# Weight conversion from 64-bit to 32-bit words: the stored width of ScalarE's part, and the engine that clamps

## The chip, the cores and the metric

One core of a Trainium2 chip runs the kernel. The metric is device microseconds of one execution. The core's engines run side by side and meet at semaphores: TensorE (matmuls and transposes, called PE in the rows, PEld for its weight loads), VectorE (DVE), ScalarE (ACT), GpSimd (POOL) and SyncE (SP), whose queue issues most of the DMAs. Each engine works its own queue in order.

## The reference

Windowed attention, then two gated expert layers one behind the other, on 2304 tokens of width 512.

```python
def attention(q, k, v):            # 4 batches, 8 heads, 576 positions, 64 wide
    scores = q @ k.T / 8           # only 0 <= row - column < 64 is kept
    return softmax(scores) @ v     # then heads side by side: x is 2304 x 512

def moe(x, w_gate, w_val, w_out):  # 512 -> 1536 -> 512
    g = x @ w_gate
    return (g * sigmoid(g) * (x @ w_val)) @ w_out

def moe2(x, w_gate, w_val, w_out):
    return (sigmoid(x @ w_gate) * (x @ w_val)) @ w_out
```

All inputs are 64-bit floats where the host hands them over as such: the weights reach the kernel as pairs of 32-bit words (`wide`), and the kernel makes 32-bit floats of them itself.

## The kernel before

The tokens are cut into five tiles of 512, 384, 512, 512 and 384 (BLOCKS, in blocks of 128). For each layer, tile and chunk `fc` of 128 of the 1536 hidden columns there are three steps, counted by `g`: the gate product (L429, 12 matmuls into bank g), the value product (L429, 12 matmuls into bank v) and the out product of the chunk before (L441, 12 matmuls). All products are made with operands split in a higher and a lower part (three terms each). Between them ScalarE makes the gate (L696, Silu or Sigmoid), VectorE multiplies (L705), ScalarE rounds the higher part of h (L707) and VectorE subtracts to get the lower one (L621), without which the out product can't go on.

What else has to be done is hung on steps in three lists, `before`, `during` and `after` a step's product: the attention of the next tile's blocks (transposes, scores, masks L263, exponentials L279, normalisation L292 to L294, and the copies kt L217, early_q L211, x L328 and L331), and the weights' conversion. The kernel's own order within these lists is the order in which each engine gets its instructions. The start, before the first product, follows a list written by hand (START), in which `ca` is round_a, `cb` is round_b, `ch` and `cl` are the split of a weight; six conversions are done in it (`ca0` to `ca5`).

There are 72 conversions of 128 x 512 weights, 36 per layer. The first layer's are due while the first token tile is multiplied, one per step; the second layer's are spread over the third and fourth tiles. One conversion goes so. SP loads 512 KB of raw words (L359). ScalarE, in round_a, scales the lower words and stores them as 16-bit integers in the first of the four 16-bit parts of a pair (L377), and stores the absolute upper word in t (L380). VectorE, in round_b, one step later, makes the second 16-bit part from sign and a constant (L388), clamps t (L389), shifts it (L390) and adds the lower word (L391). Then SP may load the next raw tile into that buffer (there are four), out weights and the second layer's go to DRAM for later tiles, and split_hi (L411, ScalarE) and split_lo (L415, VectorE) make the two parts used by the products.

Of the kernel before, what the change touches and what calls it, by code (L numbers as in the profile page):

```python
# [8 lines left out]
FP32 = mybir.dt.float32  # L9
FP32R = mybir.dt.float32r  # L10
INT32 = mybir.dt.int32
UINT32 = mybir.dt.uint32
UINT16 = mybir.dt.uint16
ACTF = mybir.ActivationFunctionType
ALU = mybir.AluOpType
# [4 lines left out]
F64_LEAST = 2.0 ** -15  # L20
F64_MOST = 122816.0
# [18 lines left out]
def attention_moe_moe(  # L40
# [20 lines left out]
    nc = tc.nc  # L61
# [7 lines left out]
    scale = 1.0 / float(D) ** 0.5  # L69
# [269 lines left out]
    raws = {}  # L339
# [22 lines left out]
    def words_of(r):  # L362
        w = r.rearrange("p (f two) -> p f two", two=2)
        half = r.bitcast(UINT16).rearrange("p (f four) -> p f four", four=4)
        return w[:, :, 0], w[:, :, 1], half[:, :, 0], half[:, :, 1], half[:, :, 3]

# [3 lines left out]
    def round_a(key):  # L372
        t = t_p.tile([128, 512], INT32, tag="t", name="t")
        mids[key] = t
        if wide:
            lower, upper, first, _, _ = words_of(raws[key])
            nc.scalar.activation(  # L377
                out=first, in_=lower.bitcast(UINT32), func=ACTF.Copy, scale=2.0 ** -29
            )
            nc.scalar.activation(out=t.bitcast(FP32), in_=upper.bitcast(FP32), func=ACTF.Abs)  # L380

    def round_b(key, keep):
        r = raws.pop(key)
        t = mids[key]
        tf = t.bitcast(FP32)
        if wide:
            lower, _, _, second, fourth = words_of(r)
            nc.vector.tensor_scalar(second, fourth, 0x8000, 0x4000, ALU.bitwise_and, ALU.bitwise_or)  # L388
            nc.vector.tensor_scalar(tf, tf, F64_LEAST, F64_MOST, ALU.max, ALU.min)  # L389
            nc.vector.tensor_scalar(t, t, 3, None, ALU.logical_shift_left)  # L390
            nc.vector.tensor_tensor(out=t, in0=t, in1=lower, op=ALU.add)  # L391
        else:
            nc.vector.tensor_copy(tf, r)
        mids[key] = tf
        if keep:
            d = dram.tile([128, 512], FP32, name=f"k{key[0]}{key[1]}{key[2]}")
            nc.sync.dma_start(out=d, in_=tf)
            kept[key] = d
# [117 lines left out]
    for b in range(B):  # L516
# [4 lines left out]
        first = {1: 12, 2: 24, 3: 46}[b]  # L521
# [29 lines left out]
    def conv_b(j):  # L551
        round_b(convs[j][1], convs[j][1][1] == "o")
        raw_ahead(j + 1 + 4)

    for j, (s, key) in enumerate(convs[SPLIT_EARLY:], SPLIT_EARLY):
        at(during, s + 1, round_a, key)
        at(during, s + 2, round_b, key, key[0] == 1 or key[1] == "o")
        at(during, s + 2, raw_ahead, j + 1 + 4)
        if key[0] == 0:
            plan_split(s + 2, key)  # L560
# [32 lines left out]
    for t in range(NTL, 2 * NTL):  # L593
        for fc in range(FC):
            n, key = SPT * t + 3 * fc + 5, (1, "o", fc)
# [29 lines left out]
    with tc.manual_schedule():  # L625
# [4 lines left out]
        t = ps_m.tile([128, 512], FP32, tag="a3", name="warm")  # L630
# [8 lines left out]
        for step in LOADS.split():  # L639
# [31 lines left out]
            "lo": lambda i: x_lo(i, x_of(0), i * 128),  # L671
            "wm": lambda k: warm(k),
            "ca": lambda j: round_a(convs[j][1]),
            "cb": lambda j: conv_b(j),
            "ch": lambda j: split_hi(convs[j][1]),
# [9 lines left out]
        for T in range(2 * NTL):  # L685
            m = T // NTL
            t = ORDER2[T - NTL] if m else T
            n = TILES[t][1]
            for fc in range(FC):
# [7 lines left out]
                    out=s, in_=gps[:, 0:n], func=(ACTF.Silu, ACTF.Sigmoid)[m]  # L697
# [54 lines left out]
```

## Time and profile before

| | |
|---|---|
| Median of three runs | 1010.43 us (1010.13 to 1010.93) |
| Profiled execution, its own time | 1010.98 us |
| Its span, first to last instruction | 1009.2 us |
| TensorE busy | 984.6 us (98%) |
| VectorE busy | 516.4 us (51%) |
| ScalarE busy | 496.7 us (49%) |
| GpSimd busy | 4.1 us, 20 instructions |

Busy times are sums over one profiled execution. TensorE's matmuls are pipelined and their ends are modelled, so its busy share says when it had work, not how well it ran. Times in a time line are microseconds from the first instruction of the span.

### The profile page before, as it was taken

Reading aid. Unit: us, or ns where it says so; the run is one execution under the profiler, and the core shown is the slowest. Engines: PE = TensorE matmul, PEld = TensorE weight load, DVE = VectorE, ACT = ScalarE, POOL = GpSimd, SP = SyncE. Lnnn points to the kernel's source line nnn. Section 1 sums busy time; section 2 is a strip of 40 time slices with the busy share of each in tenths; the row PEclk is TensorE's granted clock in tenths of the full one; section 3 lists DMA queues with packets and bytes.
Section 4 is the critical chain, followed back from the end, with each engine's and each line's share of the span. In section 5 each row is a group of like instructions: output and inputs, shape, how many; then the busy total and the mean of one; then the engine's idle time right before and its main releaser. Section 6 shows DMA issues by size and latency. Waiting matters only on the chain.

```text
span 1009.2 us, 14684 instructions
## 1 busy us (share of the span) xinstructions
PE 984.6 (98%) x5621; PEld 847.7 (84%) x5621; DVE 516.4 (51%) x1181; ACT 496.7 (49%) x981; POOL 4.1 (0%) x20
## 2 busy tenths in 40 slices
PE   8899998999999999999999999999999999999998
PEld 6677777999878788888999888899988888888997
DVE  6899994554576777767555323223322222223322
ACT  6899994655676668657444322222222222222222
POOL 1000000000000000000000000000000000000000
PEclk7799999999999999999999999999999999999999
DMA  9647798773176666573644400020020002000100
GB/s 225 187 152 214 205 234 205 196 151 108 55 223 204 203 201 223 172 233 106 210 146 146 167 1 1 1 84 1 1 73 1 1 1 73 0 1 1 42 1 32
DMA packets 164982, 113.03 MB, mean 112 GB/s; under 512 B 102704, under 2 KB 139568, under 8 KB 164912
## 3 DMA queue, kind: packets, MB, share of 16 engines
q1 hardware_dynamic: 161264, 111.18, 38.1%
q10 hardware_dynamic: 3648, 0.92, 0.4%
q8 instruction: 44, 0.72, 0.3%
q14 instruction: 26, 0.21, 0.1%
HBM read 90.05 MB, written 27.53 MB: 117 GB/s over the span
## 4 chain that ended last, share of the span: by engine, by line
PE 80%; DVE 7%; ACT 7%; issue 3%; SPq 2%; DMA 1%; DVEq 0%; ACTq 0%
PE a L441 26%; PE g L429 26%; PE v L429 24%; ACT raw L377 2%; SPq L118 2%; ACT z L279 1%; DVE raw L388 1%; PE att L244 1%; PE att L318 1%; DVE t L390 1%; PE att L302 1%; DMA ks<-in_k_dram 1%; ACT L279 1%; DVE t L389 1%; DVE s L705 1%
## 5 line engine op out<-in xcount | busy, mean ns | idle before, releaser
L429 PE MATMUL g<-x,wg 128*128 128x512 f32 (+1 forms) x1440 | 319.5, 370 | 0.7 <-ACT x L328 0.7
L429 PE MATMUL v<-x,wv 128*128 128x512 f32 (+1 forms) x1440 | 317.6, 369 | 0.0
L429 PEld LDWEIGHTS g<-x,wg 128*128 128x128 f32 x1440 | 264.6, 189 | 38.0 <-ACT x L328 0.9
L429 PEld LDWEIGHTS v<-x,wv 128*128 128x128 f32 x1440 | 261.2, 188 | 33.0
L705 DVE TENSOR_TENSOR s<-s,v 128x512 f32<-128x512 f32 (+1 forms) x120 | 75.9, 632 | 314.7 <-PE v L429 303.6
L696 ACT ACTIVATE s<-g 128x512 f32<-128x512 f32 (+1 forms) x120 | 66.7, 556 | 304.1 <-PE g L429 303.6
L441 PE MATMUL a<-h,wo 128*128 128x512 f32 (+1 forms) x720 | 164.8, 377 | 6.3 <-DVE h L621 6.3
L441 PE MATMUL a<-wo,h 128*128 128x512 f32 x648 | 157.4, 390 | 0.0
L707 ACT ACTIVATE h<-s 128x512 fp32r<-128x512 f32 (+1 forms) x120 | 70.6, 588 | 169.4 <-DVE s L705 169.3
L441 PEld LDWEIGHTS a<-h,wo 128*128 128x128 f32 x720 | 131.2, 190 | 26.5 <-DVE h L621 7.6
L441 PEld LDWEIGHTS a<-wo,h 128*128 128x128 f32 x648 | 121.3, 188 | 24.2
L377 ACT ACTIVATE raw<-raw 128x512 uint16<-128x512 uint32 x72 | 98.0, 1361 | 0.0
L621 DVE TENSOR_TENSOR h<-s,h 128x512 fp32r<-128x512 f32 (+1 forms) x120 | 76.2, 635 | 3.2
L388 DVE TENSOR_SCALAR raw<-raw 128x512 uint16<-128x512 uint16 x72 | 53.9, 748 | 17.4 <-ACT raw L377 17.3
L279 ACT ACTIVATE z<-z,nm 128x128 f32<-128x128 f32 x144 | 55.8, 390 | 2.8 <-DVE nm L263 2.7
L101 DVE TENSOR_TENSOR x<-rx,x 128x512 fp32r<-128x512 f32 (+1 forms) x20 | 12.8, 639 | 84.3 <-ACT x L100 84.3
L391 DVE CUSTOM_DVE_ANT_0 t<-raw,t 128x1024 uint16<-128x1024 uint16 x72 | 49.9, 693 | 2.5
L380 ACT ACTIVATE t<-raw 128x512 f32<-128x512 f32 x72 | 51.1, 710 | 0.0
L415 DVE TENSOR_TENSOR wo<-stay,wo 128x512 fp32r<-128x512 f32 x60 | 41.1, 685 | 0.0
L411 ACT ACTIVATE wo<-stay 128x512 fp32r<-128x512 f32 x60 | 37.4, 623 | 0.0
L415 DVE TENSOR_TENSOR wo<-tw,wo 128x512 fp32r<-128x512 f32 x48 | 32.9, 686 | 5.7 <-ACT wo L411 5.7
L389 DVE TENSOR_SCALAR t<-t 128x512 f32<-128x512 f32 x72 | 33.3, 462 | 0.0
(84 smaller groups left out, 569.4 us busy)
## 6 DMA issues: line engine op xcount, KB each, us to landing
raw<-in_moe_w_gate_dram SPq DMA_DIRECT2D x24, 512.0 KB, 4.2
raw<-in_moe_w_val_dram SPq DMA_DIRECT2D x24, 512.0 KB, 4.3
raw<-in_moe_w_out_dram SPq DMA_DIRECT2D x24, 512.0 KB, 3.7
tw<-k0o SPq DMA_DIRECT2D x48, 256.0 KB, 4.2
v<-in_v_dram SPq DMA_DIRECT2D x29, 256.0 KB, 4.6
out_dram<-o SPq DMA_DIRECT2D x18, 256.0 KB, 2.3
k<-ks SPq DMA_DIRECT2D x10, 384.0 KB, 5.4
k0o<-t SPq DMA_DIRECT2D x12, 256.0 KB, 2.3
```

The costliest lines, as they stand in the source:

```text
L279: nc.scalar.activation(out=z[:, hp, :], in_=z[:, hp, :], func=ACTF.Exp, scale=-1.0, bias=nm[:, hp:hp + 1], accum_out=su[:, hp:hp + 1],)
L377: nc.scalar.activation(out=first, in_=lower.bitcast(UINT32), func=ACTF.Copy, scale=2.0 ** -29)
L380: nc.scalar.activation(out=t.bitcast(FP32), in_=upper.bitcast(FP32), func=ACTF.Abs)
L388: nc.vector.tensor_scalar(second, fourth, 0x8000, 0x4000, ALU.bitwise_and, ALU.bitwise_or)
L391: nc.vector.tensor_tensor(out=t, in0=t, in1=lower, op=ALU.add)
L415: nc.vector.tensor_tensor(out=w[:, 1], in0=mids.pop(key), in1=w[:, 0].bitcast(FP32), op=ALU.subtract)
L429: nc.tensor.matmul(out=ps[:, 0:n], lhsT=w[:, a, c, :], rhs=xt[:, b, c, 0:n], start=(j == 0), stop=(j == len(mm) - 1),)
L441: nc.tensor.matmul(out=acc[e][:, 0:n] if m == 0 else acc[e], lhsT=w[:, a, cols] if m == 0 else h[:, a, cols], rhs=h[:, b, 0:n] if m == 0 e ...
L621: nc.vector.tensor_tensor(out=h[:, 1, 0:n], in0=s, in1=h[:, 0, 0:n].bitcast(FP32), op=ALU.subtract)
L696: nc.scalar.activation(out=s, in_=gps[:, 0:n], func=(ACTF.Silu, ACTF.Sigmoid)[m])
L705: nc.vector.tensor_tensor(out=s, in0=s, in1=vps[:, 0:n], op=ALU.mult)
L707: nc.scalar.activation(out=h[:, 0, 0:n], in_=s, func=ACTF.Copy)
```

## The change

The lower words, scaled, are stored by ScalarE over the whole 32-bit lower word, as integers of 32 bits, instead of in its lower 16 bits. The clamp of the magnitudes is taken out of VectorE's part and done by GpSimd, right behind the absolute value, with the same two bounds. VectorE's remaining three instructions stay as they were.

```diff
     def words_of(r):
         w = r.rearrange("p (f two) -> p f two", two=2)
         half = r.bitcast(UINT16).rearrange("p (f four) -> p f four", four=4)
-        return w[:, :, 0], w[:, :, 1], half[:, :, 0], half[:, :, 1], half[:, :, 3]
+        return w[:, :, 0], w[:, :, 1], half[:, :, 1], half[:, :, 3]
...
         if wide:
-            lower, upper, first, _, _ = words_of(raws[key])
+            lower, upper, _, _ = words_of(raws[key])
             nc.scalar.activation(
-                out=first, in_=lower.bitcast(UINT32), func=ACTF.Copy, scale=2.0 ** -29
+                out=lower, in_=lower.bitcast(UINT32), func=ACTF.Copy, scale=2.0 ** -29
             )
-            nc.scalar.activation(out=t.bitcast(FP32), in_=upper.bitcast(FP32), func=ACTF.Abs)
+            tf = t.bitcast(FP32)
+            nc.scalar.activation(out=tf, in_=upper.bitcast(FP32), func=ACTF.Abs)
+            nc.gpsimd.tensor_scalar(tf, tf, F64_MOST, F64_LEAST, ALU.min, ALU.max)
 
     def round_b(key, keep):
...
         if wide:
-            lower, _, _, second, fourth = words_of(r)
+            lower, _, second, fourth = words_of(r)
             nc.vector.tensor_scalar(second, fourth, 0x8000, 0x4000, ALU.bitwise_and, ALU.bitwise_or)
-            nc.vector.tensor_scalar(tf, tf, F64_LEAST, F64_MOST, ALU.max, ALU.min)
             nc.vector.tensor_scalar(t, t, 3, None, ALU.logical_shift_left)
             nc.vector.tensor_tensor(out=t, in0=t, in1=lower, op=ALU.add)
```

## Rows read from the trace of the kernel before

**Rows 1.** Busy us (instructions) by stretch; then granted clock, DMA share, GB/s.

```profile
51.80:156.00 104.20, 94.44 (x554) 75.22 (x551) 100.58 (x233) 97.34 (x173) 0.00 (x0) 0.98 0.75 207
...
175.00:265.00 90.00, 90.00 (x721) 85.56 (x720) 44.56 (x138) 48.43 (x123) 0.00 (x0) 1.00 0.55 133
...
490.00:1009.00 519.00, 515.31 (x2498) 454.90 (x2496) 164.81 (x269) 146.25 (x270) 0.00 (x0) 1.00 0.13 44
```

**Rows 2.** Waits, 51.8 to 156 us: who for whom, total us, times, longest.

```profile
PE a L441 <- DVE h L621: 6.3, 3, 2.1
...
PE att L244 <- ACT kt L217: 2.1, 2, 1.2
...
PE att L202 <- DMA q<-in_q_dram: 0.7, 1, 0.7
```

**Rows 3.** TensorE's time line around one stall: start us, us, line, operation.

```profile
58.26 2.88 PE L441 MATMUL a<-h,wo 128*128 128x512 f32 x12
60.98 2.88 PE L429 MATMUL g<-x,wg 128*128 128x512 f32 x12
...
67.63 0.71 PE L441 MATMUL a<-h,wo 128*128 128x512 f32 x2
...
74.43 2.91 PE L429 MATMUL g<-x,wg 128*128 128x512 f32 x12
```

**Rows 4.** Groups by line and shape: count, busy us, mean ns, idle before.

```profile
L377 ACT ACTIVATE raw<-raw 128x512 uint16<-128x512 uint32 x72 | 98.0, 1361 | 0.0
...
L380 ACT ACTIVATE t<-raw 128x512 f32<-128x512 f32 x72 | 51.1, 710 | 0.0
...
L388 DVE TENSOR_SCALAR raw<-raw 128x512 uint16<-128x512 uint16 x72 | 53.9, 748 | 17.4 <-ACT raw L377 17.3
...
L389 DVE TENSOR_SCALAR t<-t 128x512 f32<-128x512 f32 x72 | 33.3, 462 | 0.0
...
L390 DVE TENSOR_SCALAR t<-t 128x512 int32<-128x512 int32 x72 | 30.8, 427 | 2.5
```

**Rows 5.** ScalarE's time line, one conversion and an earlier Abs.

```profile
51.10 0.71 ACT L380 ACTIVATE t<-raw 128x512 f32<-128x512 f32 x1
...
62.50 1.36 ACT L377 ACTIVATE raw<-raw 128x512 uint16<-128x512 uint32 x1
63.60 0.71 ACT L380 ACTIVATE t<-raw 128x512 f32<-128x512 f32 x1
64.21 0.62 ACT L707 ACTIVATE h<-s 128x512 fp32r<-128x512 f32 x1
```

**Rows 6.** VectorE's time line, the same two conversions.

```profile
53.43 0.43 DVE L390 TENSOR_SCALAR t<-t 128x512 int32<-128x512 int32 x1
...
63.89 0.76 DVE L388 TENSOR_SCALAR raw<-raw 128x512 uint16<-128x512 uint16 x1
64.44 0.46 DVE L389 TENSOR_SCALAR t<-t 128x512 f32<-128x512 f32 x1
64.93 0.43 DVE L390 TENSOR_SCALAR t<-t 128x512 int32<-128x512 int32 x1
```

**Rows 7.** GpSimd's time line at the start.

```profile
1.01 0.29 POOL masks.py:199 TENSOR_SCALAR_AFFINE_SELECT ident<-ident 128x128 f32<-128x128 f32 x1
1.61 0.23 POOL L170 TENSOR_SCALAR_AFFINE_SELECT mask_n<-mask_n 64x64 f32<-64x64 f32 x1 [0.30 <-DVE mask_n L166]
...
6.11 0.52 POOL L158 MEMSET v<- 64x512 f32 x1 [1.32 <-PE att L202]
```

**Rows 8.** The chain that ended last, before the first product: start us, us, what.

```profile
35.74 1.25 ACT raw L377
...
37.92 1.23 ACT raw L377
```

**Rows 9.** TensorE's time line at the start.

```profile
26.41 1.33 PE L244 MATMUL v<-kt,early_q 64*64 64x128 f32 x10 [0.66 <-ACT early_q L211]
...
43.52 0.80 PE L429 MATMUL g<-x,wg 128*128 128x512 f32 x1 [0.70 <-ACT x L328]
```

## The prediction

> **What bounds the kernel now.** I read first the busy time by stretch, then who waited for whom, then the time lines of the engines in the stretch that these point to. By stretch [rows 1], TensorE is busy 90.00 of 90.00 us from 175 to 265 and 515.31 of 519.00 us in the last stretch: from about 160 us on its own work sets the pace, and what VectorE and ScalarE save there is worth nothing. The other row is different: from 51.8 to 156 us TensorE is busy 94.44 of 104.20 us, VectorE 100.58 and ScalarE 97.34. This is the first token tile, in which the first layer's weights are converted while they are multiplied. 29 of the 72 conversions have their VectorE part there (counted in VectorE's time line); the second layer's 36 lie later, behind a full TensorE. Time lost ahead of 160 us is not won back later, so what this stretch and the start before it lose or gain comes out at the end one to one.
>
> Who stops TensorE there [rows 2]: 6.3 of the 9.76 idle us are three waits of the out product (L441) for the lower word of h (L621, VectorE), 2.1 us are two waits for a ScalarE copy of kt (L217), and only 0.7 us is a transfer. VectorE itself hardly rests (100.58 of 104.20): its queue is simply full, and L621 stands in it behind conversions. ScalarE (97.34) is close behind it.
>
> One such stall [rows 3]: an undisturbed out product takes 2.72 us from its start to that of the next group (58.26 to 60.98). The one at 67.63 does two matmuls, waits, and the next group starts at 74.43: 6.80 us, 4.08 too many, more than the wait itself, since the matmuls behind it also run longer. For the other two I count only the wait, 2.1 us each (the row gives 6.3 for three, the longest 2.1). Together 8.3 us; with the 2.1 for kt some 10.4 us are to be had in this stretch, more if the other two stalls also slow what follows.
>
> **The change, part by part.** (1) ScalarE's store of the scaled lower words (L377) writes a 32-bit integer where it wrote 16 bits; same elements, same stride of 8 bytes. Before, it takes 1361 ns, the Abs right behind it (L380), which reads with the same stride and writes dense 32-bit words, 710 [rows 4]. In the queue they occupy 63.60 - 62.50 = 1.10 and 64.21 - 63.60 = 0.61 us [rows 5]. What makes the first so long is not shown by itself; it differs in its 16-bit type and in its strided store. Bounds for the new one: 0.61 us (as the Abs) and 1.10 (nothing gained: the stride is what costs). I take 0.61, because VectorE's own 16-bit store with this stride (L388, 748 ns) is also longer than its 32-bit neighbours of as many elements (L389 462, L390 427), so the narrow stores look like the common cause. Saving: 0.49 us of ScalarE per conversion. The Trainium skill (ScalarE: Activation LUTs, What ACT_TABLE_LOAD costs) gives an ACTIVATE with immediate scale 186 ns + 0.833 ns per element whatever the type, an estimate of 612 ns for 512 elements; L377's 1361 ns does not agree, and by that rule alone the old store would have had nothing to save.
>
> (2) The clamp leaves VectorE: L389 occupies 64.93 - 64.44 = 0.49 us of its queue [rows 6]. 29 times 0.49 is 14.2 us of VectorE in the stretch, and with (1) as much of ScalarE.
>
> (3) The clamp arrives on GpSimd, which is idle after 6.6 us. No row has a tensor_scalar there. Nearest: a memset of 512 elements 0.52 us; a select that reads and writes 64 elements 0.23 and 128 elements 0.29 [rows 7]. Carrying the select's slope (0.06 us for 64) on to 512 gives 0.65. Bounds: 0.52 (as the memset), and 512/64 x 0.23 = 1.84 (all of the select's time per element). I take 0.65, because its two sizes show that most of its time is fixed.
>
> (4) The waits. Abs, clamp and shift (L390) now pass through three engines. The shift stands in VectorE's in-order queue behind L388, and behind it stand L391, the split of another weight (L415) and then L705 or L621, for which TensorE waits. Is the clamp done in time? From the end of Abs to the start of the shift, the stretch's first conversion has 53.43 - 51.10 - 0.71 = 1.62 us; the one of 62.50 has 64.93 - 63.60 - 0.71 = 0.62 [rows 5, 6], and that is the least among the first 13, of which most have 1.4 and more, since ScalarE's part is issued one product (2.72 us) ahead. Both ends move earlier by about 0.5 us, so the gap stays: a clamp of 0.65 fits in nearly all, one of 1.84 in about a third. I cost this wait at nothing; what hides it is ScalarE's lead, and where that is gone, it costs the clamp's whole length, less what L388 covers.
>
> (5) The conversion's lower word is written whole by ScalarE, and L388 overwrites its upper half as before; L388 waited for L377 already. No DMA is added or moved. SP's loads of raw weights go out when L391 is done, so they go out earlier; the transfers' share is 0.75 over the stretch [rows 1], and a stretch shorter by 10 us raises it to some 0.83, with a full place for short times; the 0.7 us for q [rows 2] may grow, I leave 0.5 us for it.
>
> **The start.** Before the first product the chain that ended last runs through ScalarE's conversions: stores at 35.74 and 37.92 [rows 8], and before them two (the list START has ca1 and ca2) ahead of the copy early_q, for which TensorE waited 0.66 us [rows 9]. Those two save 0.98, of which that wait allows 0.66; the other two save 0.98. VectorE follows with one split less each. I take 1.6 us.
>
> **Sum.** Stretch: the stalls come from VectorE's lateness, which builds up over the conversions since the stall before: 29 over three stalls, some 10 each, are 4.9 us of relief against waits of 2.1. All would go, but the bursts of exponentials on ScalarE remain and TensorE then arrives earlier at each; I take 7 of the 10.4, and give back the 0.5 for transfers: 6.5. With 1.6 from the start 8.1 us. The profiled execution took 1010.98 us for its span of 1009.2, 0.55 above the median of the three runs shown (1010.43): 1010.43 - 8.1 = 1002.3, said as **1002**.
>
> **Rivals.** *Both engines in each other's way.* The clamp is fast and in time but VectorE loses, while it runs, what it saved. For it: VectorE is busy nearly without gaps, so that every clamp runs beside one of its operations on SBUF, two of them (L388, L390) on the same tiles' words. Against it: no row shows either engine slowing the other, GpSimd's own work ending at 6.6 us. If each clamp costs about 0.4 of its 0.65, VectorE keeps 0.1 per conversion, 2.6 us; with the start 4.2, less the transfers: **1007**. By the Trainium skill (SBUF — State Buffer, Who interferes with whom) GpSimd and VectorE share a port pair under an exclusive lock, taken by VectorE's two-port modes and two-input operations, and the second comer blocks for the whole instruction; no row here can show it.
>
> *The clamp becomes the wait.* The other side: at L390. If a clamp runs late or must itself wait for VectorE's operations to let it in, VectorE arrives at the shift and stands. L388 covers 64.44 - 63.89 = 0.55 of it [rows 6]; beyond that each 0.1 us costs 2.9 us in the stretch. It decides from the point at which VectorE loses more than the saved 0.49 plus the start's 1.6 / 29 = 0.05, that is a stall of 0.55 per conversion. At a clamp of 1.1 us (between the bounds), wholly exposed on VectorE, with 0.1 for the hand-overs: 1.2 - 0.49 - half of L388's 0.55 = 0.44 worse per conversion, 13 us; at 0.8 us, 0.14 and 4 us. In between, 8.5, and less the start's 1.6: **1017**.
>
> *The store is no cheaper.* Then ScalarE keeps its 97.34 us and becomes the limit; the start gains nothing, the stretch about half: 1010.4 - 4 = **1006**, or no change if the first rival holds too (1010).
>
> **Chances.** Forecast 0.36 (its own range 998 to 1005), hindrance 0.21 (1004 to 1010), clamp as the wait 0.25 (1012 to 1024), store no cheaper 0.13 (1004 to 1009), that and hindrance 0.05 (about 1010). A change of 0.2%, 2 us, is about what can be told from none here. Faster: 0.36 + 0.15 + 0.08 = 0.59; slower: 0.25 + 0.02 = 0.27; within: 0.14. Range: 998 leaves out little of the forecast (0.04), 1017 leaves out half of the slow rival (0.13): 998 to 1017.
>
> **What would show it.** The store's row at about 710 ns against 1361; a GpSimd row of 72 clamps near 650 ns; in the stretch 51.8 to about 148, VectorE with idle time and the three L441 waits for L621 gone or short; first product at about 42 us against 43.52. The hindrance shows as L390, L391, L415 longer than before or GpSimd rows that vary widely; the wait as idle time of VectorE before L390, ended by GpSimd. The prediction is wrong if the store stays near 1.36, or if VectorE's idle time before L390 comes to more than 0.5 us per conversion.

## The result and the profile after

| | median, us | range, runs | ratio to before, 95% |
|---|---|---|---|
| before | 1010.28 | 1009.78 to 1010.93, 4 | |
| after | 1002.32 | 999.16 to 1002.85, 4 | 0.9914 (0.9893 to 0.9936) |

The kernel is 8.0 us (0.9%) faster, at the 1002 that was forecast. The profiled execution of after took 1002.22 us, its span 1000.3 us: 8.9 less than the span before. The page of after, busy time by engine:

```profile
span 1000.3 us, 14758 instructions
...
PE 980.6 (98%) x5621; PEld 845.0 (84%) x5621; DVE 500.8 (50%) x1109; ACT 456.6 (46%) x981; POOL 58.5 (6%) x92
```

Groups by line and shape after; the new lines 390, 391, 392 and 622 are 388, 390, 391 and 621 of before, 382 is the clamp on GpSimd:

```profile
L390 DVE TENSOR_SCALAR raw<-raw 128x512 uint16<-128x512 uint16 x72 | 57.2, 795 | 9.0 <-ACT raw L377 9.0
...
L382 POOL TENSOR_SCALAR t<-t 128x512 f32<-128x512 f32 x72 | 54.5, 756 | 415.3 <-ACT t L381 369.3 <-DMA k1g<-t 9.5 <-DMA v<-in_v_dram 8.6
L622 DVE TENSOR_TENSOR h<-s,h 128x512 fp32r<-128x512 f32 x72 | 52.0, 722 | 3.2
...
L381 ACT ACTIVATE t<-raw 128x512 f32<-128x512 f32 x72 | 47.9, 665 | 0.2 <-DVE wo L416 0.2
L377 ACT ACTIVATE raw<-raw 128x512 int32<-128x512 uint32 x72 | 47.8, 665 | 0.0
...
L391 DVE TENSOR_SCALAR t<-t 128x512 int32<-128x512 int32 x72 | 32.5, 451 | 9.0 <-POOL t L382 9.0
```

The store fell from 1361 ns [rows 4] to 665, as the Abs beside it. The clamp takes 756 ns on average, and the VectorE lines got longer by 24 to 47 ns. VectorE's idle time ahead of L390 halved, from 17.4 us [rows 4] to 9.0, but 9.0 us ahead of the shift L391, ended by GpSimd, are new.

Busy time by stretch (as [rows 1]; the third stretch holds the second layer's conversions), and who stopped TensorE from the first product to that of the second token tile (42 to 165 us):

```profile
51.80:156.00 104.20, 97.36 (x580) 77.62 (x572) 99.07 (x208) 85.41 (x178) 24.08 (x29) 1.00 0.80 217
...
262.00:481.00 219.00, 218.41 (x1336) 178.24 (x1335) 149.77 (x341) 132.74 (x287) 25.03 (x36) 1.00 0.61 194
```
```profile
PE a L442 <- DVE h L622: 5.5, 3, 2.1
PE att L202 <- DMA q<-in_q_dram: 1.3, 2, 1.1
PE att L202 <- DMA k<-in_k_dram: 0.8, 2, 0.5
```

VectorE is as full as before (99.07 of 104.20 us), ScalarE is not (85.41 against 97.34). The three waits for h are still there, 5.5 us where [rows 2] has 6.3. The 2.1 us for ScalarE's copy of kt are gone, and transfers for q and k have come up to 2.1 us.

TensorE's time line at the first product and at the first of the three stalls, to be held against [rows 9] and [rows 3]:

```profile
42.10 4.21 PE L430 MATMUL g<-x,wg 128*128 128x512 f32 x9 [0.69 <-ACT x L328]
...
69.03 2.56 PE L442 MATMUL a<-h,wo 128*128 128x512 f32 x10 [1.79 <-DVE h L622]
71.43 2.88 PE L430 MATMUL g<-x,wg 128*128 128x512 f32 x12
```

The first product comes 1.4 us earlier. The ten matmuls behind the stall take 2.56 us and the next group starts 2.40 us after them; before, 4 us passed there. From here on I cut the span at three marks, taken from TensorE's time line: the first gate product, the first gate product of the second token tile, and the two products between which the second layer's conversions lie.

| span in us, of one profile each | start | first tile | second layer | rest |
|---|---|---|---|---|
| before | 43.5 | 128.2 | 221.5 | 616 |
| after | 42.1 | 122.7 | 219.3 | 616 |

So 1.4 + 5.5 + 2.2 = 9.1 us, less 0.2 lost in the rest: the second layer, which the prediction had at nothing, gave a quarter. TensorE's granted clock (1.00 stands for 2.4 GHz, 0.50 for 1.2) was 0.72 in the start and 0.96 in the first tile of before, 0.73 and 0.98 in after.

### The profile page after: what moved, and what is told of

It is laid out like the page before. It is cut to its first block, busy times and chain, and to the rows that moved or that the text cites. A ratio compares the mean times of both kernels' runs of the same rounds, so it can differ in the third digit from the quotient of the medians.

```text
span 1000.3 us, 14758 instructions
## 1 busy us (share of the span) xinstructions
PE 980.6 (98%) x5621; PEld 845.0 (84%) x5621; DVE 500.8 (50%) x1109; ACT 456.6 (46%) x981; POOL 58.5 (6%) x92
## 3 DMA queue, kind: packets, MB, share of 16 engines
q1 hardware_dynamic: 161264, 111.18, 38.4%
## 4 chain that ended last, share of the span: by engine, by line
PE 84%; DVE 8%; DMA 2%; issue 2%; ACT 2%; SPq 1%; POOL 0%; DVEq 0%; POOLq 0%; ACTq 0%
PE a L442 26%; PE g L430 26%; PE v L430 26%; DVE raw L390 2%; PE att L244 1%; PE att L318 1%; PE att L302 1%; ACT z L279 1%; DVE z L263 1%; DVE t L391 1%; DVE t L392 1%; DVE h L622 1%; DMA k<-ks 1%; DVE wo L416 1%; DMA raw<-in_moe_w_val_dram 0%
## 5 line engine op out<-in xcount | busy, mean ns | idle before, releaser
L442 PE MATMUL a<-h,wo 128*128 128x512 f32 (+1 forms) x720 | 162.1, 373 | 5.5 <-DVE h L622 5.5
L622 DVE TENSOR_TENSOR h<-s,h 128x512 fp32r<-128x512 f32 (+1 forms) x120 | 78.5, 655 | 3.2
L382 POOL TENSOR_SCALAR t<-t 128x512 f32<-128x512 f32 x72 | 54.5, 756 | 415.3 <-ACT t L381 369.3
L390 DVE TENSOR_SCALAR raw<-raw 128x512 uint16<-128x512 uint16 x72 | 57.2, 795 | 9.0 <-ACT raw L377 9.0
L381 ACT ACTIVATE t<-raw 128x512 f32<-128x512 f32 x72 | 47.9, 665 | 0.2 <-DVE wo L416 0.2
L377 ACT ACTIVATE raw<-raw 128x512 int32<-128x512 uint32 x72 | 47.8, 665 | 0.0
L391 DVE TENSOR_SCALAR t<-t 128x512 int32<-128x512 int32 x72 | 32.5, 451 | 9.0 <-POOL t L382 9.0
```

Source lines behind the costliest of these rows:

```text
L381: nc.scalar.activation(out=tf, in_=upper.bitcast(FP32), func=ACTF.Abs)
L382: nc.gpsimd.tensor_scalar(tf, tf, F64_MOST, F64_LEAST, ALU.min, ALU.max)
L442: nc.tensor.matmul(out=acc[e][:, 0:n] if m == 0 else acc[e], lhsT=w[:, a, cols] if m == 0 else h[:, a, cols], rhs=h[:, b, 0:n] if m == 0 e ...
L622: nc.vector.tensor_tensor(out=h[:, 1, 0:n], in0=s, in1=h[:, 0, 0:n].bitcast(FP32), op=ALU.subtract)
```

## The experiments

The first four kernels of the table ran on one chip, the next three on another, the last four on a third, with runs of before beside them (1010.36, 1010.56 and 1010.42 us); medians of different chips are less comparable than those of one. The start, the first tile, the second layer and the granted clock (in the start, then in the first tile) are read from each kernel's one profile.

| kernel | median, us | range, runs | ratio (95%) | start | first tile | second layer | clock |
|---|---|---|---|---|---|---|---|
| store only | 1001.79 | 1001.14 to 1003.19, 4 | 0.9913 (0.9896 to 0.9929) | 40.2 | 126.6 | 218.6 | 0.87, 0.95 |
| clamp only | 1008.75 | 1006.38 to 1011.66, 10 | 0.9984 (0.9973 to 0.9995) | 42.2 | 126.5 | 222.0 | 0.95, 0.95 |
| no clamp | 995.7 | 992.3 to 996.64, 4 | 0.9849 (0.9829 to 0.9869) | 39.7 | 120.5 | 218.5 | 0.83, 0.96 |
| two clamps | 1016.58 | 1015.38 to 1016.68, 4 | 1.0059 (1.0044 to 1.0074) | 41.1 | 131.5 | 224.2 | 0.83, 0.94 |
| START's clamps on VectorE | 1002.76 | 1001.62 to 1003.71, 4 | 0.9926 (0.9911 to 0.994) | 40.2 | 125.8 | 219.3 | 0.84, 0.96 |
| only START's on GpSimd | 1000.74 | 999.97 to 1004.97, 4 | 0.9917 (0.989 to 0.9944) | 40.7 | 123.7 | 218.6 | 0.87, 0.97 |
| store in layer 1 only | 1004.01 | 1001.94 to 1008.75, 8 | 0.9942 (0.9925 to 0.9958) | 40.8 | 123.7 | 221.6 | 0.79, 0.97 |
| after again | 1000.38 | 1000.05 to 1001.15, 4 | 0.9899 (0.9886 to 0.9913) | 38.4 | 124.3 | 219.3 | 1.00, 0.96 |
| store only again | 1003.96 | 1002.53 to 1005.51, 5 | 0.9932 (0.9916 to 0.9947) | 40.2 | 128.4 | 218.6 | 0.84, 0.93 |
| after, earlier q and k | 1000.91 | 998.83 to 1003.39, 6 | 0.9904 (0.9887 to 0.9921) | 42.0 | 123.7 | 219.3 | 0.73, 0.97 |
| store only, earlier q and k | 1002.52 | 999.54 to 1004.95, 6 | 0.9917 (0.9897 to 0.9937) | 39.0 | 123.7 | 218.6 | 0.91, 0.97 |

**The store alone.** The 32-bit store, the clamp left on VectorE:

```diff
-            nc.gpsimd.tensor_scalar(tf, tf, F64_MOST, F64_LEAST, ALU.min, ALU.max)
...
+            nc.vector.tensor_scalar(tf, tf, F64_LEAST, F64_MOST, ALU.max, ALU.min)
```

> The 32-bit store on ScalarE alone; the clamp stays on VectorE as before. Theory (VectorE's full queue sets the first tile; the store helps the start and little else): first product about 1.4 us earlier, the three waits for L621 still about 2 us each, VectorE's conversion rows as before (462 ns for the clamp); 1010.3 - 1.5 to 2.5 = 1008 to 1009. Rival (ScalarE's bursts were the cause of the stalls, the clamp's move only moves VectorE's time to a shared path): most of the gain is here, 1003 to 1005.

Measured 1001.79 us: alone it gives as much as the whole change did beside its own runs of before (ratios 0.9913 and 0.9914). The theory that hung the gain on VectorE missed; the rival, for which ScalarE's relief carries it, came nearer and was still too high. Its waits of TensorE, 41 to 156 us, and the second layer's stretch:

```profile
PE a L442 <- DVE h L622: 6.3, 3, 2.1
...
PE att L244 <- ACT kt L217: 0.2, 1, 0.2
```
```profile
262.00:481.00 219.00, 218.92 (x1342) 179.18 (x1341) 160.10 (x379) 133.25 (x293) 0.00 (x0) 1.00 0.62 193
```

The waits for h are what they were (6.3 us, three): VectorE got no relief. The waits for kt fell from 2.1 us [rows 2] to 0.2. And the second layer became 2.9 us shorter. How, the trace of before shows. Its windows, VectorE's waits (160 to 500 us), and the time lines of VectorE and TensorE at one place:

```profile
268.00:490.00 222.00, 220.25 (x1341) 179.59 (x1340) 160.19 (x378) 153.93 (x290) 0.00 (x0) 1.00 0.61 191
```
```profile
DVE raw L388 <- ACT raw L377: 15.5, 12, 1.8
```
```profile
270.48 0.76 DVE L388 TENSOR_SCALAR raw<-raw 128x512 uint16<-128x512 uint16 x1 [1.69 <-ACT raw L377]
...
274.12 0.16 DVE L292 TENSOR_SCALAR su<-su 128x4 f32<-128x4 f32 x1
```
```profile
275.37 0.63 PE L302 MATMUL att<-ident,z 128*128 128x128 f32 x4 [0.61 <-DVE z L294]
```

VectorE, in order, stands 1.69 us before L388 for the long store, though it is far from full; what is queued behind it, the scaling of the softmax (L292 to L294), comes late, and TensorE waits 0.61 us for z. TensorE's idle time in the stretch went from 222.00 - 220.25 = 1.75 us to 219.00 - 218.92 = 0.08; VectorE's waits for the store went from 15.5 to 7.9 us. That is 1.7 of the 2.9 us; the rest stands in TensorE's busy time, whose ends are modelled, and was not followed up.

**The clamp alone.** The 16-bit store with the clamp on GpSimd:

```diff
+            first = raws[key].bitcast(UINT16).rearrange("p (f four) -> p f four", four=4)[:, :, 0]
...
-                out=lower, in_=lower.bitcast(UINT32), func=ACTF.Copy, scale=2.0 ** -29
+                out=first, in_=lower.bitcast(UINT32), func=ACTF.Copy, scale=2.0 ** -29
```

> The clamp on GpSimd alone; ScalarE stores 16 bits as before. Theory: the start gains little (0 to 0.5 us), the first tile gains what VectorE keeps (about 0.25 us per conversion, 29 of them), as far as ScalarE, at 1.10 us per store, lets it: 1004 to 1007. Rival: nothing or a loss, since GpSimd gets its input no earlier and VectorE is held up by it: 1009 to 1012.

1008.75 us, 1.6 faster than before: less of a gain than the theory had for it, and just outside the rival's range. The wait for h is not less than before (6.5 us in three, 41 to 160 us), and the second layer is 222.0 us, no better. The first tile is as short as with the store alone (126.5 and 126.6 us, both at a clock of 0.95), and no wait of TensorE for kt is left (0.2 us with the store alone). Groups by shape:

```profile
L378 ACT ACTIVATE raw<-raw 128x512 uint16<-128x512 uint32 x72 | 98.0, 1361 | 0.0
...
L383 POOL TENSOR_SCALAR t<-t 128x512 f32<-128x512 f32 x72 | 56.8, 788 | 420.9 <-ACT t L382 382.1 <-DMA v<-in_v_dram 7.1 <-DMA k1g<-t 6.5
```

**No clamp, and two.** The changed kernel without the clamp (no bounds on the magnitudes are applied), and with the clamp done twice on GpSimd:

```diff
-            nc.gpsimd.tensor_scalar(tf, tf, F64_MOST, F64_LEAST, ALU.min, ALU.max)
```
```diff
             nc.gpsimd.tensor_scalar(tf, tf, F64_MOST, F64_LEAST, ALU.min, ALU.max)
+            nc.gpsimd.tensor_scalar(tf, tf, F64_MOST, F64_LEAST, ALU.min, ALU.max)
```

> The changed kernel without any clamp (left out: the bounds on the magnitudes). Theory (a clamp running on GpSimd lengthens VectorE's operations beside it, about 0.25 us per conversion in the trace after): VectorE's rows fall back to 748, 427, 693 ns, the waits for L621 shrink, 2 to 4 us faster than the changed kernel: 998 to 1000. Rival (the lengthening falls where VectorE would have waited anyway): as the changed kernel, 1001 to 1003.

> The changed kernel with the clamp done twice on GpSimd (the second changes nothing in the result). Theory: VectorE loses about 0.25 us more per conversion and waits at the shift (L391) more often; the gain of the change is halved or lost: 1006 to 1012. Rival (GpSimd's work is hidden): as the changed kernel, 1001 to 1003.

Without it 995.7 us, below what the theory had, and 6.1 less than the store alone on the same chip: that is the whole worth of taking the clamp off VectorE. VectorE's busy time is 486.3 us where after has 500.8, so each of the 72 clamps takes 14.5 / 72 = 0.20 us from VectorE although it runs on GpSimd. The first tile, where VectorE is full, counts for itself. Its windows with the store alone, after and without a clamp, and VectorE's waits for the clamp there (after, 41 to 165 us):

```profile
40.22:166.79 126.57, 118.52 (x700) 94.33 (x701) 114.06 (x270) 94.48 (x193) 0.00 (x0) 0.95 0.79 209
...
42.10:164.75 122.65, 114.94 (x700) 91.58 (x701) 109.33 (x238) 94.02 (x193) 24.70 (x30) 0.98 0.79 213
...
39.73:160.19 120.46, 115.98 (x700) 93.35 (x701) 101.19 (x238) 93.66 (x193) 0.00 (x0) 0.96 0.83 220
```
```profile
DVE t L391 <- POOL t L382: 1.5, 3, 0.5
```

Without a clamp VectorE is busy 12.9 us less than with the clamp on VectorE (114.06 against 101.19). With the clamp on GpSimd 8.1 of these come back (109.33), 0.27 for each of 30 clamps, and 1.5 are waits at the shift: some 3 us of relief are left. TensorE's waits without the clamp, 41 to 160 us:

```profile
PE att L202 <- DMA q<-in_q_dram: 3.6, 1, 3.6
PE a L441 <- DVE h L621: 0.6, 1, 0.6
```

The wait for h has all but gone, and the load of q has become the wait. With two clamps 1016.58 us, 14 to 16 more than after: more than I expected. Groups by shape there (383 is the second clamp):

```profile
L383 POOL TENSOR_SCALAR t<-t 128x512 f32<-128x512 f32 x72 | 53.4, 741 | 6.0
L382 POOL TENSOR_SCALAR t<-t 128x512 f32<-128x512 f32 x72 | 53.3, 741 | 371.2 <-ACT t L381 371.2
L392 DVE TENSOR_SCALAR t<-t 128x512 int32<-128x512 int32 x72 | 39.3, 546 | 24.0 <-POOL t L383 24.0
```

VectorE now stands 24.0 us ahead of the shift and loses 512.7 - 486.3 = 26.4 us of busy time besides: the two rivals of the prediction at twice the dose. By the prediction the change turns to a loss where VectorE loses 0.55 us per conversion. Two clamps take (26.4 + 24.0) / 72 = 0.70 from it, and the kernel is slower than before; one takes (14.5 + 9.0) / 72 = 0.33.

**The operations by themselves.** A kernel that runs only the store in six forms, and VectorE's operations alone (6 times) and beside a row of 12 clamps; nothing else of the kernel is computed:

```diff
+            lambda: nc.scalar.activation(out=f1, in_=lo1.bitcast(UINT32), func=ACTF.Copy, scale=2.0 ** -29),
+            lambda: nc.scalar.activation(out=lo2, in_=lo2.bitcast(UINT32), func=ACTF.Copy, scale=2.0 ** -29),
...
+        clamp = lambda: nc.gpsimd.tensor_scalar(gt, gt, 122816.0, 2.0 ** -15, ALU.min, ALU.max)
...
+            lambda: nc.vector.tensor_tensor(out=va, in0=va, in1=vb, op=ALU.subtract),
+            lambda: nc.vector.tensor_tensor(out=va, in0=va, in1=ps, op=ALU.mult),
```

> Not the reference's computation: it times the disputed operations by themselves, 6 or 12 of each in a row, and writes ones as its output. ScalarE's store: if the 16-bit width with a stride is what costs, 16 bits with stride 8 bytes 1360 ns also into another tile, 16 bits dense and 32 bits with either stride 610 to 710; if the conversion to integers costs, all integer forms are long. GpSimd: the clamp alone about 610 ns each. VectorE beside a row of clamps: if the two share a path, the forms with two SBUF inputs or in a fast mode become longer by several hundred ns each and the clamps too, while the form with a PSUM input stays at 685 ns; if not, all stay as alone.

Groups by shape, the stores (lines 53 to 58 are the six forms, 58 the absolute value; 53, 55 and 56 write 16 bits, 56 to 58 densely):

```profile
L53 ACT ACTIVATE r<-r 128x512 uint16<-128x512 uint32 x6 | 8.1, 1344 | 2.6 <-DMA r<-in_moe_w_gate_dram 2.5
...
L55 ACT ACTIVATE r<-r 128x512 uint16<-128x512 uint32 x6 | 8.0, 1332 | 0.2
...
L54 ACT ACTIVATE r<-r 128x512 int32<-128x512 uint32 x6 | 4.0, 659 | 0.2
L56 ACT ACTIVATE d<-r 128x512 uint16<-128x512 uint32 x6 | 4.0, 659 | 0.2
L57 ACT ACTIVATE d<-r 128x512 int32<-128x512 uint32 x6 | 3.9, 656 | 0.2
```

16 bits dense cost 659 ns, 32 bits with the stride 659, only 16 bits with the stride of 8 bytes 1332 to 1344. Then VectorE's operations, by windows with one operation each: two inputs in SBUF (the memory that holds the tiles) alone and beside the clamps, with the clamps' row, and the same with one input in PSUM (where TensorE's products land):

```profile
L68 DVE TENSOR_TENSOR va<-va,vb 128x512 f32<-128x512 f32 x6 | 4.1, 691 | 0.2
...
L68 DVE TENSOR_TENSOR va<-va,vb 128x512 f32<-128x512 f32 x12 | 11.5, 956 | 0.4
L63 POOL TENSOR_SCALAR gt<-gt 128x512 f32<-128x512 f32 x12 | 11.2, 937 | 1.5 <-DVE gt L80 0.5
...
L69 DVE TENSOR_TENSOR va<-va,ps 128x512 f32<-128x512 f32 x6 | 4.1, 686 | 0.2
...
L69 DVE TENSOR_TENSOR va<-va,ps 128x512 f32<-128x512 f32 x12 | 8.2, 687 | 0.4
L63 POOL TENSOR_SCALAR gt<-gt 128x512 f32<-128x512 f32 x12 | 7.4, 614 | 1.5 <-DVE gt L80 0.5
```

With both inputs in SBUF, VectorE's operation goes from 691 to 956 ns and the clamp from 614 to 937; with one in PSUM neither moves. The 16-bit operation of L390 went from 737 to 996 ns, the shift from 427 to 690, each with one input. In the changed kernel the same shows in single instructions, on GpSimd's and VectorE's time lines:

```profile
50.41 0.61 POOL L382 TENSOR_SCALAR t<-t 128x512 f32<-128x512 f32 x1 [8.66 <-ACT t L381]
...
55.30 1.09 POOL L382 TENSOR_SCALAR t<-t 128x512 f32<-128x512 f32 x1 [1.05 <-ACT t L381]
```
```profile
55.83 1.10 DVE L622 TENSOR_TENSOR h<-s,h 128x512 fp32r<-128x512 f32 x1
```

Undisturbed 0.61 and 0.69 us, here 1.09 and 1.10. Which operations meet agrees with the Trainium skill (SBUF — State Buffer, Who interferes with whom), as far as a VectorE operation with two SBUF inputs contends with GpSimd and one with a PSUM input does not. That the pair is an exclusive lock, on which the second comer blocks for the whole instruction, does not agree: both get longer here, and a pair takes some 0.95 us where one after the other would take 0.61 + 0.69 = 1.30.

**Which conversions, where.** START's six clamps on VectorE with the rest on GpSimd (the condition below), the reverse (the condition without its not), and the 32-bit store for the first layer alone (clamps on VectorE):

```diff
+            if not early[0]:
+                nc.gpsimd.tensor_scalar(tf, tf, F64_MOST, F64_LEAST, ALU.min, ALU.max)
```
```diff
+                out=lower if key[0] == 0 else first, in_=lower.bitcast(UINT32), func=ACTF.Copy, scale=2.0 ** -29
```

> The changed kernel with the clamp of START's six conversions on VectorE and the other 66 on GpSimd. Revised theory (the store pays at the start, 3.3 us, in the first tile with the clamp's move, 4 us or more, and 2 to 3 us in the second layer; GpSimd's clamps take back 1.9 us at the start): 3.3 + 4 + 2 to 3 = 9 to 10 us below before, 1000 to 1001.5, first product near 40.2. Rival (the differences at the start are chance from one execution to the next): as the changed kernel, about 1002, first product anywhere from 40 to 42.

> The other half: START's six clamps on GpSimd, the other 66 on VectorE. Revised theory: first product near 42.1, the stretch as with the store alone (three waits for L621 of 2.1 us): 1003 to 1005, the slowest of the versions with the 32-bit store. Rival (chance at the start): as the store alone, 1001.5 to 1002.5.

> The 32-bit store in the first layer's 36 conversions only, the 16-bit one in the second layer's 36; all clamps on VectorE. Theory (in the second layer VectorE waited for the long store, the normalisation and with it TensorE's transposes came late): 2 to 3 us slower than the store alone in both layers, 1004 to 1005. Rival (behind 160 us nothing counts, as the prediction had it): as the store alone, about 1002.

The theory that START's clamps decide the start fell: the first product comes at 40.2 and 40.7 us, with no order in it, and the medians, 1002.76 and 1000.74 us, overlap in their ranges. The third came as its theory had it (1004.01) and settles the second layer: with the 16-bit store there it takes 221.6 us, as before (221.5), where the 32-bit store has 218.6 in four kernels.

**After and the store alone, again, on one chip, and with q and k loaded earlier.** The last edit moves a first-turn load four products ahead:

```diff
-            at(during, base - 2, load_qk, i)
+            at(during, base - (6 if i < TURN else 2), load_qk, i)
```

> The changed kernel once more, beside the store alone on the same chip. Theory (on top of the store the clamp's move pays next to nothing: what VectorE saves is half lost beside GpSimd, and the rest meets a late transfer): within 1.5 us of the store alone. Rival (the clamp's move pays 2 us or more): 999 to 1000.5 where the store alone is at 1002.

> The store alone once more: 1001 to 1002.5 by either theory; it is the measure for the changed kernel and for the two versions with earlier loads.

> The changed kernel with the next tile's q and k loaded six steps ahead of their block instead of two (blocks below TURN only). Theory (with the store and the moved clamp the first tile's end meets q's transfer, 1.1 us in the trace after): TensorE's waits for q and k gone, 1 to 2 us faster than the changed kernel: 1000 to 1001. Rival (the transfers' engines are full there, an earlier load only delays the raw weights): no faster, 1002 to 1003.

> The store alone with the same earlier loads. Theory: no wait for q or k stands in that trace, so nothing to gain: within 0.8 us of the store alone. If this one gains as much as the changed kernel does by the earlier loads, it is not the moved clamp that runs into the transfer.

Here the clamp's move is worth 1003.96 - 1000.38 = 3.6 us, which the theory had not: its rival comes nearer, though the store alone was slower than expected of it. The two first measurements, on different chips, gave nothing (1001.79 against 1002.32), and the two versions that differ from this pair in START's six conversions alone gave the reverse on one chip (1000.74 with the other 66 clamps on VectorE, 1002.76 with them on GpSimd). The earlier loads took the waits for q and k (2.1 us) out of after's list, but 1000.91 against 1000.38 us is no gain, as the rival had it: 1.3 us for kt and 0.8 for x (L331), as much again, stood there instead. Beside the store alone, 1002.52 against 1003.96, the ranges overlap.

Why do equal kernels differ by 3 us? One cause is seen at the stalls. Windows of the ten matmuls behind each of the three waits for h, store alone:

```profile
65.60:69.50 3.90, 3.90 (x11) 3.04 (x12) 3.83 (x8) 2.12 (x5) 0.00 (x0) 0.59 0.71 206
107.20:111.20 4.00, 3.97 (x10) 3.18 (x11) 3.93 (x8) 2.21 (x5) 0.00 (x0) 0.57 0.73 216
148.85:153.30 4.45, 4.45 (x11) 3.48 (x12) 3.23 (x7) 2.24 (x5) 0.00 (x0) 0.50 1.04 292
```

After waits of 2.1 us the granted clock was 0.50 to 0.59, that is all or most of the stretch at 1.2 GHz instead of 2.4, and the ten matmuls took 4.1 to 4.6 us. In before the same happened at the first and third stall (0.57, 0.65) and not at the second (1.00), after a wait of 2.12 us; in the changed kernel, after 1.79, 2.06 and 1.66 us, at none.

The clock column of the table shows how much of the spread goes with this. With the 32-bit store and the first tile's clamps on VectorE, the first tile took 123.7 us at 0.97 (three profiles), 126.6 at 0.95 and 128.4 at 0.93; with the clamps on GpSimd 122.7 at 0.98, 123.7 at 0.97, 124.3 and 125.8 at 0.96. At one clock, then, it does not show which engine clamps. The start goes the same way: with the 32-bit store and its clamps on either engine, 42.1 and 42.0 us at 0.73, 40.8 at 0.79, 40.2 to 40.7 at 0.84 to 0.87, 39.0 at 0.91, 38.4 at 1.00.

## Why the prediction was right

The total, 8.1 us forecast and 8.0 measured, is right in part by luck. The largest term, 6.5 us, was to come mostly from the waits for h that VectorE's relief would remove; these gave 0.8. The rest of the stretch's 5.5 us came from other waits and from the clock, and 2.2 us came from the second layer, which the sum had at nothing.

**The store (step 1): right in size, its reason half right.** 665 ns against the 0.61 taken for the queue (in after's queue it occupies 0.54). The narrow type was named as the common cause; the operations by themselves show that it takes the narrow type and the stride together.

**The clamp's relief (step 2): mis-sized.** 29 times 0.49 = 14.2 us were to leave VectorE in the stretch. In the first tile each clamp takes 0.27 back by contention and 1.5 / 30 = 0.05 as wait, so that about 0.1 is left, some 3 us; VectorE stayed full and the waits for h went from 6.3 to 5.5 us (4.7 in the second profile), not away. Without any clamp they are 0.6: the sum's reasoning about them holds once the relief is real. The hindrance rival, which let VectorE keep 0.1 per conversion, 2.6 us, is therefore what VectorE did; its 1007 missed because it gave the store nothing beyond the start.

**The clamp's duration (step 3): right undisturbed.** Taken 0.65; 614 ns alone, 756 on average beside VectorE.

**The wait before the shift (step 4): nearly right.** Costed at nothing; 9.0 us in all, 18 waits of at most 0.5 of which three lie in the first tile, against the 0.5 us per conversion named as the sign of a wrong prediction. What it costs if the cover is gone, two clamps show.

**The stretch (sum): right to 1 us by other parts.** 6.5 forecast, 5.5 in the profiles. The wait for x in before (43 to 172 us), one of the parts below:

```profile
PE att L202 <- DVE x L331: 0.8, 1, 0.8
```

The parts: 0.8 from the waits for h, 2.1 from kt (the store alone leaves 0.2 of it, the clamp alone none), some 2.7 because no stall was followed by a low clock (4 against 2.4 us at the first, 3.57, at a clock of 0.65, against 2.46 at the third), 0.8 from a wait of TensorE for x (L331) that the list of before has and that of after hasn't, less 1.2 of longer waits for q and k, where 0.5 was put: 5.2. The part of the clock is no work of the change that these runs show: the changed kernel had 0.98 in the first tile of one profile and 0.96 in that of the other, and before had 0.96.

**"From 160 us on worth nothing": wrong.** TensorE's full row hid 1.75 us of waits, and the store was worth 2.9 us there; the clamp on GpSimd takes 0.7 back (219.3 against 218.6, in four profiles each). These 2.2 us make up for what the stretch, at 5.5, fell short.

**The start: right at the clock of before's profile.** 1.6 forecast; at a clock of 0.72 to 0.73 the first product comes 1.4 and 1.5 us earlier (43.5 against 42.1 and 42.0). At a higher clock the store is worth more: 42.2 us with the 16-bit store at 0.95, 39.0 with the 32-bit store at 0.91. The changed kernel itself starts at 42.1 and 38.4, and of before there is one profile.

**The shares.** The sum gave ScalarE and VectorE equal savings and hung the stretch on VectorE. The runs give the store nearly all: 6.5 to 8.6 us by itself, the clamp by itself 1.6, and on top of the store between 2.0 lost and 3.6 gained. That last range stays open; it is the size of the spread between executions.

## What to carry to other kernels

A stretch in which TensorE reads as full can still hold a per cent of waits: list the waits there before calling a saving elsewhere worthless. Moving an operation between VectorE and GpSimd saves only what is left after each has slowed the other on SBUF; measure the pair, and keep the moved work on GpSimd beside VectorE operations that read PSUM. A store that is both narrow and strided is worth widening where the rest of the word is free.

## What the runs showed of the hardware

The 16-bit store with a stride of 8 bytes costs ScalarE twice the time (1344 against 659 ns) where neither narrowness nor stride alone costs anything. The rule that the prediction weighed (the Trainium skill, ScalarE: Activation LUTs, What ACT_TABLE_LOAD costs: an estimate of 612 ns for 512 elements; the page says fp32 and bf16 alike, the prediction took it for any type) comes within 50 ns of the other forms run by themselves, but not of this one. GpSimd and VectorE lengthen each other on SBUF, by 0.27 and 0.32 us on 0.69 and 0.61, without excluding each other. And the same program starts at different clocks: windows of 20 to 30 us, of after and of its repetition:

```profile
20.00:30.00 10.00, 9.24 (x73) 7.13 (x72) 8.75 (x37) 8.01 (x28) 2.02 (x3) 0.50 1.02 246
```
```profile
20.00:30.00 10.00, 5.37 (x92) 4.45 (x94) 9.69 (x36) 9.54 (x32) 1.68 (x3) 1.00 1.14 262
```

At 1.2 GHz TensorE was busy 9.24 of 10 us and the first product came at 42.1; at 2.4 GHz 5.37, and it came at 38.4. What set the clock there was not found.
